# The filter's spectrum in a convolution kernel: its stores move to GpSimd's queue, its swapped copy is made in two halves

## The chip, the cores and the metric

The kernel runs on one core of a Trainium2 chip. The metric is the device time of one execution in microseconds (us), here the median of three runs. One further execution was recorded by the hardware profiler; the traces and pages below are of that one.

## The reference

A long convolution along the sequence by FFT, and then a block that mixes tokens by phases. Batch 8, sequence S = 5696, width 128:

```
Y  = rfft(x, 2S, axis=1) * rfft(h, 2S, axis=0)[None]
y  = irfft(Y, 2S, axis=1)[:, :S]                  # the convolution, 8 x 5696 x 128
theta = y @ w_theta;  zr, zi = y*cos(theta), y*sin(theta)
u  = y + einsum('ts,bsd->btd', w_tok_r, zr) + einsum('ts,bsd->btd', w_tok_i, zi)
out = u + max(u @ w_ch, 0)
```

`w_tok_r` and `w_tok_i` are 5696 x 5696 float32; most of the kernel's time is the product with them.

## The kernel before

The first 365 us or so are the convolution. It works on 8 groups, one after the other: group g is a pair of batches (`bp = g // 2`) and one half of the 128 columns (`dh = g % 2`). Each group goes through four stages, which are woven: stage A of group g+1 runs beside stage C of group g, and stage B of group g+1 beside stage D of group g.

- **Stage A** (`stage_a`) is the first short transform of x, by matmul with the table `f1_t`; ScalarE (L259) or VectorE (L257) evict it into the tile `a`. The pool of `a` has one buffer, so `a` of group 1 (a__1403 in the trace) is written where the filter's spectrum (a__241) was.
- **Stage B** (`stage_b`) runs over 12 chunks of 8 (the last: 2) rows of the first transform. TensorE makes the second transform of a chunk (`f2`, L270), ScalarE evicts it as `xs` (L431, two buffers), and VectorE multiplies it with the filter's spectrum into `uv_t` (L433, or two products at L438 in group 0 and for the short chunk). The spectrum comes in the tile `hs`, four buffers (`LEAD = 4`): `load(c + LEAD)` is issued once chunk c has been multiplied.
- **Stage C** and **stage D** transform back; VectorE and ScalarE evict them as `g` (L460, L458) and `yt` (L493, L495). SyncE stores `yt` to DRAM in eight pieces (L502).

The filter h goes the same way first. Its spectrum, `hst_of(c)`, stays in SBUF in place of its own `a`, with real rows on partitions 0 to 63 and imaginary rows on 64 to 127, for both halves of the columns. Group 0 multiplies by it directly, and by `hs`, in which the two row blocks have been exchanged by a copy from SBUF (L421, two copies of 64 KB for a chunk). The groups from 1 on can't, since the SBUF room goes to `a` of the next group. They read `hf_hbm` in DRAM (L423, 256 KB for a chunk), whose layout is (chunk, column half, 128 rows, straight or exchanged, 512). It is filled in two steps:

- `h_store(n)`, n = 0 to 11, one call behind each of group 0's stage B chunks in program order, writes 64 rows of SBUF (L369): for chunks 0 to 5, 6 to 10 and 11, for each column half and each of real and imaginary. The pieces are 384, 320 and 16 KB. They make rows 0 to 63.
- `swap_rows()` fills rows 64 to 127 with the same data exchanged, by six copies from DRAM to DRAM (L406). Each covers both column halves; with chunk and half merged, the first dimension of the copies is 12, 10 and 2.

Both are issued by SyncE, whose order is made by the scheduler, as is TensorE's: L369, the first L406, group 0's L421 from chunk 4 on, the other L406, the L423 of group 1. VectorE, ScalarE and GpSimd keep the program's order up to the end of group 0's stage C (`ordered`). GpSimd issues the loads of x (L153: 16 pieces for a group, of 160 and 18 KB, each group's loads two groups ahead; from group 2 on, a copy at L151 makes a piece wait for that group's `g`).

A table of sines and cosines for stage D (`e_table`) is made in three parts. ScalarE's two activations of the first part (L195 and L202, called `curves()`) stand behind chunk 5 of group 0's stage B.

The second part of the kernel, from about 365 us on, forms the phases and multiplies by the two large matrices (L1334 and L1234 on TensorE), whose rows GpSimd loads in a ring (L680).

Of the kernel before, what the change touches and what calls it, by code (L numbers as in the profile page):

```python
# [22 lines left out]
def kernel(  # L23
# [10 lines left out]
    nc = tc.nc  # L34
# [63 lines left out]
    hf_hbm = nc.dram_tensor("hf_hbm", (NCK, 2, P, 2, HD * CK), F16, kind="Internal").ap()  # L98
# [5 lines left out]
    def psum():  # L104
        return fp.tile([P, 2, 512], F32, tag="ps", name="ps")
# [244 lines left out]
    def hst_of(c, n=1):  # L350
        c0 = CHK[c][0]
        c1 = CHK[c + n - 1][0] + CHK[c + n - 1][1]
        return a_h["a"].rearrange("p (h k) d -> p h (k d)", h=2)[:, :, c0 * HD:c1 * HD]
# [12 lines left out]
    def h_store(i):  # L366
        i, h, ri = i // 4, i // 2 % 2, i % 2
        c0, c1, w = ((0, NCK // 2, HD * CK), (NCK // 2, NCK - 1, HD * CK), (NCK - 1, NCK, HD * CHK[-1][1]))[i]
        nc.sync.dma_start(hf_hbm[c0:c1, h, :64, ri, :w].rearrange("c p n -> p c n"),  # L369
                          hst_of(c0, c1 - c0)[64 * ri:64 * ri + 64, h].rearrange("p (c n) -> p c n", n=w))  # L370

    r_u = fc.tile([P, P], F16)
    r_v = fc.tile([P, RC], F16)
# [24 lines left out]
            cosine(e_t[:K1, n0:n0 + 11, 0, :], k3)  # L398
        return curves

    def swap_rows():
        for c0, c1, w in ((0, NCK // 2, HD * CK), (NCK // 2, NCK - 1, HD * CK), (NCK - 1, NCK, HD * CHK[-1][1])):
            for ri in range(2):
                dst, src = (hf_hbm[c0:c1, :, r0:r0 + 64, r, :w].rearrange("c h p n -> (c h) p n")
                            for r0, r in ((64, ri), (0, 1 - ri)))
                nc.sync.dma_start(dst, src)  # L406

    def e_minus():
        nc.vector.tensor_scalar(e_neg[:K1], e_t[:K1, 1:2 * NP:2], -1.0, None, op0=mult)
# [1 line left out]
    def stage_b(a_st, dh, warm=WARM, first=False):  # L411

        hs_of = {}

        def load(c):
            if c >= NCK:
                return
            hs = hs_of[c] = fh.tile([P, 2, HD * CK], F16, tag="hs", name="hs")
            w = HD * CHK[c][1]
            for e in range(2 if first else 0):  # L420
                nc.sync.dma_start(hs[64 * e:64 * e + 64, 1, :w], hst_of(c)[64 - 64 * e:128 - 64 * e, dh])  # L421
            if not first:
                nc.sync.dma_start(hs[:, :, :w], hf_hbm[c, dh, :, :, :w])  # L423

        def chunk(c):
            c0, ck = CHK[c]
            hv = hs_of[c][:, :, :HD * ck].rearrange("p r (d k) -> p r d k", k=ck)
            straight = hst_of(c)[:, dh].rearrange("p (d k) -> p d k", k=ck).unsqueeze(1) if first else hv[:, 0:1]
            ps = f2(a_st, c, warm)
            xs = fs.tile([P, 2, HD, CK], F16, tag="xs", name="xs")  # L430
            nc.scalar.activation(xs[:, :, :, :ck], ps, AF.Copy)  # L431
            if ck == CK and not first:
                nc.vector.tensor_tensor(  # L433
                    uv[:, :, :, c0:c0 + ck],
                    xs.rearrange("p e d k -> p e (d k)").unsqueeze(1).to_broadcast([P, 2, 2, HD * CK]),
                    hv.rearrange("p r d k -> p r (d k)").unsqueeze(2).to_broadcast([P, 2, 2, HD * CK]), op=mult)
            for r in range(2 if ck < CK or first else 0):
                nc.vector.tensor_tensor(  # L438
                    uv[:, 2 * r:2 * r + 2, :, c0:c0 + ck], xs[:, :, :, :ck],
                    (hv[:, 1:2] if r else straight).to_broadcast([P, 2, HD, ck]), op=mult)  # L440
            load(c + LEAD)
        return [lambda c=c: load(c) for c in range(LEAD)], [lambda c=c: chunk(c) for c in range(NCK)]

    def stage_c(st, last):

        def chunk(q):
            if q == 0:
                st["g"] = fg.tile([P, 2 * N2, P], F16, tag="g", name="g_")
            ps = psum()
            for i in range(8):  # L450
                o = ps[:, i // 4, (i % 4) * P:(i % 4 + 1) * P]
                at = (q + i) * K1
                nc.tensor.matmul(o, u_t[:, at:at + P], r_u, start=True, stop=False)  # L453
                nc.tensor.matmul(o[:, 2 * NP:], v_t[:, at:at + P], r_v, start=False, stop=True)  # L454
            g_out = st["g"][:K1, :, q:q + 8]
            g_in = ps[:K1].rearrange("p a (q c) -> p c (a q)", q=4)
            if (last and q % 24 == 0) or (not last and q % 32 == 16):
                nc.scalar.activation(g_out, g_in, AF.Copy)  # L458
            else:
                nc.vector.tensor_copy(g_out, g_in)  # L460
        return [lambda q=q: chunk(q) for q in range(0, 2 * HD, 8)]
# [48 lines left out]
    def front(g, by_dve=(), a_=None, spare=None):  # L510
        if g >= len(groups):
            return [], [], []
        bp, dh = groups[g]
        x16 = x16s[g].rearrange("p b n d -> p (b n) d")
        steps, a_st = stage_a(lambda q: x16[:NB, :, q], by_dve, a_, spare)
        return (steps, *stage_b(a_st, dh, 0 if g else WARM // 2, g == 0))
# [141 lines left out]
    def open_ring():  # L658

        ring["all"] = keep.tile([P, K1 * 3 * N2], BF16, tag="keep", name="ring")  # L660
        pump()
# [109 lines left out]
    def with_load(step, load):  # L771
        def both():
            step()
            if load:
                ring["upto"] += 1
                pump()
        return both

    for g, (bp, dh) in enumerate(groups):
        st = {}  # L780
        last = g + 1 == len(groups)
        a_, load_, b_ = fronts.pop(g + 1) if g + 1 in fronts else front(g + 1)
        if last:
            for _ in range(3):
                steps0.pop(0)()
        now = ([with_load(steps0.pop(0), n < 6) for n in range(9)] if last else [], 0.0, 0.88)
        c_ = stage_c(st, last)
        if g == 0:
            ec = []
            swap_rows()  # L790
            now = ([lambda: ec.append(e_table(1)), lambda: ec.pop()(), lambda: ec.append(e_table(2)), lambda: ec.pop()(),
                    e_minus],
                   -0.1, 0.6)
        woven((c_, 0.06 if a_ else 0.0, 1.0), (a_, 0.0, 0.88), now, load_, (load_x(g + 2, st), 0.1, 1.02))
        if g == 0:
            ordered.close()
        if g + 2 == len(groups):
            xin.close()
            open_phases()
            load_ya0()  # L800
        now = [steps0.pop(0) for _ in range(4)] if last else []
        woven((b_, 0.0, 0.8), (stage_d(st, bp, dh, load_ya1 if last else None, g + 2 == len(groups)), 0.08 if b_ else 0.0, 1.1 if b_ else 1.0), now)
        if g + 2 == len(groups):
            load_ya1(st["yt"], True)
            open_ring()
# [332 lines left out]
    for i, (k, p, tt, j0, s0, nj) in enumerate(stretches):  # L1138
# [47 lines left out]
        if tt is None:  # L1186
# [21 lines left out]
            if end_of_pair:  # L1208
# [5 lines left out]
                c, c0 = c_last  # L1214
# [184 lines left out]
```

## Time and profile before

| | us |
|---|---|
| runs | 2031.64, 2032.19, 2037.83 (median 2032.19) |
| profiled execution | 2035.47, its span 2033.7 |
| TensorE busy | 1956.1 (96%) |
| VectorE busy | 1538.2 (76%) |
| ScalarE busy | 636.9 (31%) |
| GpSimd busy | 974.6 (48%) |

Rows of the trace give a start in us from the span's beginning, a duration, the engine, the line of the kernel, the operation and its tiles (out<-in), and in brackets how long the engine had stood idle and what ended that. PE is TensorE, DVE VectorE, ACT ScalarE, POOL GpSimd; SPq is SyncE's queue of DMA issues. A DMA issue has a duration on its queue, and later a landing. The clock in a table of windows is the share of full speed that TensorE was granted.

### The profile page before, as it was taken

The numbers are of one execution on the slowest core, as the hardware profiler recorded it, in microseconds if no ns is written. First come the engines' busy times: TensorE is split into PE (matmuls) and PEld (weight loads), VectorE is DVE, ScalarE is ACT, GpSimd is POOL, SyncE is SP. The second block draws the span as 40 slices with busy tenths as digits, with TensorE's granted clock in tenths as the row PEclk, the third lists the DMA queues.
The fourth block names the chain that finished last, engine by engine and source line by source line (L and its number), as shares of the span: only waits on it lengthen the run. The fifth ranks groups of instructions, "written<-read, shape, count | busy, mean of one in ns | idle before, by whom it ended". The sixth has DMA issues, their size and how long they took to land.

```text
span 2033.7 us, 42627 instructions
## 1 busy us (share of the span) xinstructions
PE 1956.1 (96%) x16297; PEld 1079.9 (53%) x16297; DVE 1538.2 (76%) x2819; ACT 636.9 (31%) x934; POOL 974.6 (48%) x1787
## 2 busy tenths in 40 slices
PE   7799998989999999999999999999999999999998
PEld 5689887644444444444444444444444444444444
DVE  8877787666778787887867668768677786777767
ACT  6777788852233323333300000011111111111111
POOL 8323313575363635454566555453545445354450
PEclk9998999999999999999999999999999999999999
DMA  9999987999798989999999799886978879788793
GB/s 153 161 165 150 152 174 212 254 227 193 152 181 172 178 169 161 185 170 177 168 172 156 119 246 223 133 153 125 153 133 146 150 123 157 129 150 143 133 158 84
DMA packets 508525, 332.48 MB, mean 163 GB/s; under 512 B 186727, under 2 KB 461671, under 8 KB 508231
## 3 DMA queue, kind: packets, MB, share of 16 engines
q0 software_dynamic: 322656, 157.47, 61.0%
q1 hardware_dynamic: 179680, 160.74, 27.2%
q10 hardware_dynamic: 5984, 11.54, 1.6%
q8 instruction: 128, 2.10, 0.4%
q14 instruction: 77, 0.63, 0.1%
HBM read 373.24 MB, written 92.95 MB: 229 GB/s over the span
## 4 chain that ended last, share of the span: by engine, by line
PE 65%; DMA 4%; DVE 2%; POOL 1%; issue 1%; ACT 0%; DVEq 0%; ACTq 0%
PE m L1334 61%; DMA ring<-in_moe_w_tok_i_dram 2%; POOL ring L680 1%; PE v L993 1%; PE utp L986 1%; DVE c L1341 1%; PE m L1338 1%; DVE wt L906 1%; DMA ring<-in_moe_w_tok_r_dram 1%; PE theta_ps L564 0%; PE tpz L934 0%; DMA wl<-in_moe_w_tok_i_dram 0%; DVE b L844 0%; DMA cp_hbm<-c 0%; PE m L1201 0%
## 5 line engine op out<-in xcount | busy, mean ns | idle before, releaser
L680 POOL DMA_DIRECT2D ring<-in_moe_w_tok_i_dram x720 | 387.7, 545 | 675.5 <-DVE wt L906 578.2
L906 DVE STREAM_TRANSPOSE wt<-ring 128x384 f32<-128x384 f32 (+2 forms) x720 | 359.0, 523 | 125.0 <-PE m L1334 77.0
L680 POOL DMA_DIRECT2D ring<-in_moe_w_tok_r_dram x720 | 386.3, 547 | 119.2 <-DVE wt L906 68.3
L1334 PE MATMUL m<-b,wt 128*128 128x512 bf16 x1640 | 388.3, 379 | 1.9 <-DVE wt L906 1.7
L1334 PEld LDWEIGHTS <-wt 128*128 128x128 bf16 x1804 | 176.0, 98 | 215.5 <-DVE wt L906 4.3
L1341 DVE TENSOR_TENSOR c<-c,m 128x512 f32<-128x512 f32 x412 | 265.2, 668 | 0.4 <-PE m L1334 0.4
L988 ACT ACTIVATE ring<-utp 128x512 bf16<-128x512 bf16 x85 | 50.7, 597 | 572.0 <-PE utp L986 572.0
L453 PE MATMUL ps<-r_u,uv_t 128*128 128x128 f16 x1024 | 117.4, 220 | 5.6 <-DVE g__1416 L460 2.0
L1234 PE MATMUL m<-b,wt 128*128 128x512 bf16 x480 | 114.2, 386 | 7.7 <-DMA b<-zz 5.4
L983 ACT ACTIVATE ub<-c 128x512 bf16<-128x512 f32 x88 | 55.2, 628 | 199.7 <-DVE c L1295 118.9
L454 PE MATMUL ps<-r_v,uv_t 128*128 128x100 f16 x1024 | 115.5, 209 | 0.1
L153 POOL DMA_DIRECT2D x<-in_x_dram x128 | 98.1, 773 | 20.7 <-POOL x L151 14.9
L454 PEld LDWEIGHTS <-uv_t 128*128 128x128 f16 x1024 | 100.8, 99 | 7.0 <-issue 5.9
L433 DVE TENSOR_TENSOR uv_t<-xs,hs 128x2048 f16<-128x2048 f16 x77 | 91.5, 1221 | 17.1 <-ACT xs L431 9.8
L453 PEld LDWEIGHTS <-uv_t 128*128 128x128 f16 x1024 | 100.8, 98 | 1.6 <-DVE uv_t L438 1.3
L431 ACT ACTIVATE xs<-ps 128x1024 f16<-128x1024 f32 x96 | 90.7, 972 | 29.2 <-PE ps L270 15.2
L1234 PEld LDWEIGHTS <-wt 128*128 128x128 bf16 x528 | 51.0, 99 | 67.1 <-issue 12.4
L566 ACT ACTIVATE red<-theta_ps,magic 128x512 f32<-128x512 f32 (+1 forms) x46 | 31.6, 687 | 153.1 <-PE theta_ps L564 92.9
L270 PEld LDWEIGHTS <-w_t 64*128 64x128 f16 x3240 | 56.5, 98 | 32.6 <-issue 24.3
L936 ACT ACTIVATE ring<-tpz 128x512 bf16<-128x512 bf16 (+1 forms) x46 | 27.4, 597 | 137.0 <-PE tpz L934 122.5
L250 PE MATMUL ps<-f_t,x 89*128 89x180 f16 x512 | 64.5, 258 | 0.7 <-DVE a L257 0.5
L995 DVE SCALAR_TENSOR_TENSOR c<-v,c 128x512 f32<-128x512 f32 x88 | 59.8, 682 | 2.8 <-PE v L993 2.1
(2932 smaller groups left out, 3765.3 us busy)
## 6 DMA issues: line engine op xcount, KB each, us to landing
ring<-in_moe_w_tok_r_dram POOLq DMA_DIRECT2D x352, 96.0 KB, 4.6
ring<-in_moe_w_tok_i_dram POOLq DMA_DIRECT2D x352, 96.0 KB, 4.9
ring<-in_moe_w_tok_r_dram POOLq DMA_DIRECT2D x352, 80.0 KB, 4.5
ring<-in_moe_w_tok_i_dram POOLq DMA_DIRECT2D x352, 80.0 KB, 4.0
cp_hbm<-c SPq DMA_DIRECT2D x88, 256.0 KB, 2.4
c<-cp_hbm SPq DMA_DIRECT2D x88, 256.0 KB, 3.7
out_dram<-c SPq DMA_DIRECT2D x88, 256.0 KB, 4.3
hs<-hf_hbm SPq DMA_DIRECT2D x77, 256.0 KB, 3.6
```

The source lines that it names most:

```text
L153: nc.gpsimd.dma_start(x16[p0:p1, e, n0:n0 + 16, :HD], bass.AP(tensor=src.tensor, offset=src.offset + (p0 * N2 + n0) * D + dh * HD, ap=[[N2 ...
L250: nc.tensor.matmul(ps[:, i // 2, (i % 2) * 2 * K1:(i % 2 + 1) * 2 * K1], lhs(q + i), f1_t[:NB], start=True, stop=True)
L431: nc.scalar.activation(xs[:, :, :, :ck], ps, AF.Copy)
L433: nc.vector.tensor_tensor(uv[:, :, :, c0:c0 + ck], xs.rearrange("p e d k -> p e (d k)").unsqueeze(1).to_broadcast([P, 2, 2, HD * CK]), hv. ...
L453: nc.tensor.matmul(o, u_t[:, at:at + P], r_u, start=True, stop=False)
L454: nc.tensor.matmul(o[:, 2 * NP:], v_t[:, at:at + P], r_v, start=False, stop=True)
L680: nc.gpsimd.dma_start(wb[32 * i:32 * i + 32, :ng, :nj * 64], bass.AP(tensor=a.tensor, offset=a.offset + row0 * S + p * H + i * QR + j0 * 6 ...
L906: nc.vector.transpose(wt.rearrange("p j t r -> p (j t r)").bitcast(F32).rearrange("p (j g t) -> p g j t", j=TJ, g=4)[:, :ng, :nj], wb[:, : ...
L995: nc.vector.scalar_tensor_tensor(c[:m], v[:m], 0.0, c[:m], op0=ALU.max, op1=ALU.add)
L1234: nc.tensor.matmul(ms[n // 2 * 2 + h], a[n][:, j, :, r], bts_of[p][jj][n % 2 * 2 + h][:, r, :], start=(n % 2 == 0 and jj == 0 and r == 0), ...
L1334: nc.tensor.matmul(ms[q], a[q][:, j, :, r], bts[jj][q][:, r, :], start=(jj == 0 and r == 0), stop=(jj == NJ - 1 and r == 1 and q not in left))
L1341: nc.vector.tensor_tensor(c, z, ms[q], op=op)
```

## The change

GpSimd, and no longer SyncE, issues the twelve stores of `h_store`. In its program order they stand behind the loads of x for group 1 and the making of the identity, and ahead of the loads of x for group 2. `swap_rows` takes a column half: half 1, which group 1 reads, is called at the beginning of group 0's loop step, half 0, which group 2 reads, at that of group 1's. The copies of each are held in SyncE's order behind the load of `hs` that was issued last by then (`tc.issue_after`): chunk 11 of group 0 for half 1, chunk 11 of group 1 for half 0. There are twelve copies of half the size in place of six; their first dimension is 6 or 5, and for the last chunk 64.

```diff
     def h_store(i):
...
-        nc.sync.dma_start(hf_hbm[c0:c1, h, :64, ri, :w].rearrange("c p n -> p c n"),
-                          hst_of(c0, c1 - c0)[64 * ri:64 * ri + 64, h].rearrange("p (c n) -> p c n", n=w))
+        nc.gpsimd.dma_start(hf_hbm[c0:c1, h, :64, ri, :w].rearrange("c p n -> p c n"),
+                            hst_of(c0, c1 - c0)[64 * ri:64 * ri + 64, h].rearrange("p (c n) -> p c n", n=w))
...
-    def swap_rows():
+    hs_last = {}
+
+    def swap_rows(h):
         for c0, c1, w in ((0, NCK // 2, HD * CK), (NCK // 2, NCK - 1, HD * CK), (NCK - 1, NCK, HD * CHK[-1][1])):
             for ri in range(2):
-                dst, src = (hf_hbm[c0:c1, :, r0:r0 + 64, r, :w].rearrange("c h p n -> (c h) p n")
-                            for r0, r in ((64, ri), (0, 1 - ri)))
-                nc.sync.dma_start(dst, src)
+                dst, src = (hf_hbm[c0:c1, h, r0:r0 + 64, r, :w] for r0, r in ((64, ri), (0, 1 - ri)))
+                with tc.issue_after(hs_last["load"]):
+                    nc.sync.dma_start(dst, src)
...
             for e in range(2 if first else 0):
-                nc.sync.dma_start(hs[64 * e:64 * e + 64, 1, :w], hst_of(c)[64 - 64 * e:128 - 64 * e, dh])
+                hs_last["load"] = nc.sync.dma_start(hs[64 * e:64 * e + 64, 1, :w],
+                                                    hst_of(c)[64 - 64 * e:128 - 64 * e, dh]).ins
             if not first:
-                nc.sync.dma_start(hs[:, :, :w], hf_hbm[c, dh, :, :, :w])
+                hs_last["load"] = nc.sync.dma_start(hs[:, :, :w], hf_hbm[c, dh, :, :, :w]).ins
...
         c_ = stage_c(st, last)
+        if g == 1:
+            swap_rows(0)
         if g == 0:
             ec = []
-            swap_rows()
+            swap_rows(1)
```

## The prediction

> **What bounds the kernel now.** I read the page first. Its chain of work that ended last begins at 529 us and is matmul time almost throughout:
>
> ```profile
> PE 65%; DMA 4%; DVE 2%; POOL 1%; issue 1%; ACT 0%; DVEq 0%; ACTq 0%
> ```
>
> The change lies in the first 130 us, ahead of that chain. There each stage waits for the one before it, so a stall counts at the end only if it delays the hand-over from group to group; I take one that does to move all that follows. I went to VectorE's timeline (start, duration, what runs, idle time and its releaser):
>
> ```profile
> 54.27 0.69 DVE L438 TENSOR_TENSOR uv_t<-xs,a__241 128x1024 f16<-128x1024 f16 x1
> 58.61 0.69 DVE L438 TENSOR_TENSOR uv_t<-xs,hs 128x1024 f16<-128x1024 f16 x1 [3.64 <-DMA hs<-a__241]
> ...
> 60.48 0.69 DVE L438 TENSOR_TENSOR uv_t<-xs,a__241 128x1024 f16<-128x1024 f16 x1
> ...
> 88.18 1.22 DVE L460 CAST g__1416<-ps 90x1024 f16<-90x1024 f32 x1 [0.38 <-PE ps L454]
> 90.91 1.08 DVE L493 CAST yt<-ps 128x890 bf16<-128x890 f32 x1 [1.51 <-PE ps L489]
> 91.92 2.35 DVE L433 TENSOR_TENSOR uv_t<-xs,hs 128x2048 f16<-128x2048 f16 x2
> ...
> 129.18 1.22 DVE L460 CAST g__2476<-ps 90x1024 f16<-90x1024 f32 x1 [0.38 <-PE ps L454]
> 130.82 2.36 DVE L433 TENSOR_TENSOR uv_t<-xs,hs 128x2048 f16<-128x2048 f16 x2 [0.41 <-ACT xs L431]
> ```
>
> In group 0 VectorE stands 3.64 us for chunk 4's copy into hs, though chunk 0 freed that buffer at 50.64 (its second product starts at 49.95 and takes 0.69). SyncE's own queue shows why:
>
> ```profile
> 33.66 18.43 SPq L369 DMA_DIRECT2D hf_hbm<-a__241  x12
> 52.14 0.90 SPq L406 DMA_DIRECT2D hf_hbm<-hf_hbm  x1
> 53.14 12.18 SPq L421 DMA_DIRECT2D hs<-a__241  x16
> 65.36 8.37 SPq L406 DMA_DIRECT2D hf_hbm<-hf_hbm  x5
> 73.84 35.20 SPq L423 DMA_DIRECT2D hs<-hf_hbm  x16
> ```
>
> The twelve stores of the spectrum hold the queue until 52.1 and a 768 KB swap goes ahead, so chunk 4's copy is issued at 53.14 behind that swap's data.
>
> **The change part by part.** *Stores off SyncE.* Chunk 4's two copies can go out at 50.7 and 51.3 (0.595 us each, the median of L421). Landing took 1.7 to 4.6 us over all L421, so the second lands between 53.0 and 55.9; VectorE needs it at 54.9. Between nothing and 1 us of the wait is left. But ScalarE is next in line:
>
> ```profile
> 54.42 1.02 ACT L431 ACTIVATE xs<-ps 128x1024 f16<-128x1024 f32 x1 [0.18 <-DVE uv_t L438]
> 55.34 1.10 ACT L195 ACTIVATE e_t<-e_turns,zero_b 90x979 f16<-90x979 f32 x1
> 56.35 1.11 ACT L202 ACTIVATE e_t<-e_t,half_pi 90x979 f16<-90x979 f32 x1
> 59.42 1.02 ACT L431 ACTIVATE xs<-ps 128x1024 f16<-128x1024 f32 x1 [1.96 <-DVE uv_t L438]
> ```
>
> The sine and cosine stand in ScalarE's fixed order between chunk 5 and chunk 6. Chunk 6's eviction cannot start before about 57.4 and ends at 58.4; VectorE's chunk 6 then starts at 58.4 instead of 60.48. The gain is 2.05 us, not 3.64: the table replaces the DMA. It also covers the remaining 0 to 1 us of the copy's wait.
>
> *Stores on GpSimd.* It is free where they land in its order:
>
> ```profile
> 46.02 0.29 POOL masks.py:199 TENSOR_SCALAR_AFFINE_SELECT ident_bf<-ident_bf 128x128 bf16<-128x128 bf16 x1
> 71.06 0.18 POOL L151 COPY x<-g__1416 1x1 f16<-1x1 f16 x1 [24.75 <-DVE g__1416 L460]
> ...
> 91.28 4.41 POOL L153 DMA_DIRECT2D x<-in_x_dram  x7 [0.21 <-issue]
> ```
>
> Twelve issues at 0.60 (the 9-row pieces of x) to 0.91 us (the 80-row pieces) are 7 to 11 us inside 24.75 us of idleness; the x pieces behind them are not delayed. The stores begin 12.6 us later than now, at 46.3. Their 2.88 MB went at about 270 GB/s between 48 and 52 us, and beside 1 MB of hs copies end near 46.3 + 3.9/0.27 = 61. What waits for that is ScalarE's first write of the next `a` (67.08 now, 65 then), which reuses the buffer they read. Margin 4 us: cost nothing; if the cover is gone, a stall of ScalarE one for one.
>
> [...] The row at 91.28 is 0.63 us per issue while VectorE runs L433, 2048 elements in 1.22 us, twice the rate per element of L460 (1024 in 1.22); elsewhere the same pieces take 0.60. [...]
>
> *The swap in halves.* Each half is 1.44 MB, with first dimension 6 or 5 chunks where it was 12 or 10. The DMA view from 69 to 73 us has the end of the 12-block copy, then the 10-block one (busy tenths of the 16 engines, GB/s):
>
> ```profile
> DMA  6887888878878866856957767668568567676676
> GB/s 246 307 307 256 307 297 287 297 276 287 307 266 287 297 246 236 287 205 246 430 205 256 256 225 256 236 225 287 205 225 287 205 246 266 225 256 236 225 256 236
> ```
>
> First about 0.75 at 290, then 0.62 at 245: twelve and ten sixteenths, 24.5 GB/s per leading block. So I estimate 147 and 123 GB/s for 6 and 5 blocks, 2.7 us per big copy and 10.7 us per half, where the whole now takes about 11. [...]
>
> The first half goes out near 62 and ends near 75; the hs loads behind it are needed at 90. Cost nothing. The second half sits in SyncE's order as one copy behind group 1's last hs load (105), then the eight yt stores (107.4 to 112.5), then the other five, and only then group 2's first four hs loads, which now go out by 109. In them, each of the first five engines moves 192 KB of big swaps and 64 KB of hs after 112.5: 10.4 us at 24.5 KB/us alone, to 123. But x loads run from 113 on. If the queue gets 55% (an estimate: x moves 160 KB every 2.2 us here, 73 GB/s, and up to 160 GB/s at 91 us), it is 18.9 us: the first hs lands at 129 to 130, the fourth at 132. VectorE wants the first at 130.9 and the others 1.2 us apart. Cost: nothing by a hair; bounds 0 and 4.5 us (at 10.6 KB/us per engine: 250 GB/s from 38 to 46 us, less x's 81, over 16).
>
> *Order.* The built program's instruction lists differ elsewhere in one place: in group 2's stage B, VectorE takes the yt copy ahead of its first two products, and ScalarE one too, as group 1 does now. From the last g copy's start to the end of stage B group 1 takes 108.70 − 88.18 = 20.52, less 1.21 of DMA waits 19.3; group 2 takes 147.92 − 129.18 = 18.74. Cost 0.57; with the waits 1.8.
>
> *Sum.* −2.05 + 0.57 = −1.5 us. On the profiled execution's 2035.47 (span 2033.7) that is 2034.0. That execution lies 3.3 above the median of 2032.19, so the prediction for a median is 2030.7.
>
> **The rivals.** *The halves run on too few engines (slower).* Group 2's hs comes late by 3.6 to 4.5 us, and PE then sits idle. The windows grant PE 0.50 after such gaps (106 to 113, 174 to 185 us); in group 1 the third g copy comes 7.17 us after stage B's end, in group 2, without it, 4.42: 2.75 more. Total −1.5 + 4.5 + 2.75 = +5.8 or 2038, up to 2041 if a second group is drawn in. It decides once the fourth swap copy ends after about 127. For it: 0.62 busy, and a margin of 1 us. Against: x fills half the capacity only. Chance 0.30, of which 0.19 beyond 0.3%.
>
> [...] Chance 0.07.
>
> *More than one stall goes (faster).* Group 1's 1.21 us of hs waits and its half-clock stretch (2.75) vanish with the earlier hand-over, and the new order costs nothing: −2.05 − 1.21 − 2.75 = −6.0, and another group's stretch could go too: 2026. For it: the stretches come in some groups only and not in others alike. Chance 0.17.
>
> *It does not do what it says.* The stores' data, now beside the copies, hold chunk 4 as long as the swap did: no gain, 2032 to 2034. Against it: 4.6 us is the slowest L421. Chance 0.08.
>
> **How the numbers follow.** My forecast keeps 0.38. A measurement of this kernel can tell about 0.3% (6.1 us) from no change, since three runs spread over 6.2 us. Slower: 0.19 + 0.06 + 0.02 = 0.27; faster 0.17; same 0.38 + 0.11 + 0.01 + 0.06 = 0.56. Range 2024 to 2040: it holds the forecast's bounds (2.05 at best, 4.5 lost), most of the few-engine case and most of the faster one. The forecast alone would be 2028 to 2034.
>
> **What would show it.** Right: chunk 4's copies issued by 51, no DMA wait of over 1 us ahead of chunk 4's second product, chunk 6 at 58.4 behind the cosine, stage B ending near 65.3; 12 L369 rows on GpSimd between 46 and 61; swap copies at 5 to 6 sixteenths of the engines. Wrong: a DMA wait of L433 in group 2, a store landing after 65, or the clock's 0.50 stretches in other groups than now by more than one.

## The result, and the profile after

The changed kernel is slower: 2040.61 us median of 11 runs (2034.06 to 2049.31) against 2031.87 of 11 runs of the kernel before beside them (2025.72 to 2037.83). The ratio is 1.0056, 95% interval 1.0039 to 1.0072: 8 to 15 us, more than the 0.3% that can be told apart. The profiled execution took 2048.64 (span 2046.9) and is among the slowest of its runs, so its 13.2 us more of span are not the mean loss. Lines of the kernel have moved by two to five: L421 is now L423, L423 is L426, L406 is L408, L433 is L436, L438 is L441, L431 is L434, L460 is L463, L493 is L496, L453 is L456, L502 is L505.

The chain that ended last is what it was, matmuls of the second part:

```profile
PE 66%; DMA 3%; DVE 3%; issue 1%; POOL 1%; ACT 0%; ACTq 0%; DVEq 0%; SPq 0%; POOLq 0%
```

VectorE's timeline of the changed kernel in group 0 and in group 2 (start, duration, what runs, in brackets the idle time ahead of it and its releaser):

```profile
53.92 0.69 DVE L441 TENSOR_TENSOR uv_t<-xs,a__241 128x1024 f16<-128x1024 f16 x1
59.74 0.69 DVE L441 TENSOR_TENSOR uv_t<-xs,hs 128x1024 f16<-128x1024 f16 x1 [5.13 <-DMA hs<-a__241]
60.35 0.69 DVE L441 TENSOR_TENSOR uv_t<-xs,a__241 128x1024 f16<-128x1024 f16 x1
62.25 0.69 DVE L441 TENSOR_TENSOR uv_t<-xs,hs 128x1024 f16<-128x1024 f16 x1 [1.22 <-DMA hs<-a__241]
...
133.49 1.08 DVE L496 CAST yt<-ps 128x890 bf16<-128x890 f32 x1 [1.45 <-PE ps L492]
138.04 2.36 DVE L436 TENSOR_TENSOR uv_t<-xs,hs 128x2048 f16<-128x2048 f16 x2 [3.47 <-DMA hs<-hf_hbm]
140.84 2.36 DVE L436 TENSOR_TENSOR uv_t<-xs,hs 128x2048 f16<-128x2048 f16 x2 [0.44 <-ACT xs L434]
144.49 1.23 DVE L436 TENSOR_TENSOR uv_t<-xs,hs 128x2048 f16<-128x2048 f16 x1 [1.29 <-DMA hs<-hf_hbm]
146.64 4.82 DVE L436 TENSOR_TENSOR uv_t<-xs,hs 128x2048 f16<-128x2048 f16 x4 [0.92 <-DMA hs<-hf_hbm]
```

The wait for chunk 4's copy, 3.64 before, has not gone: it is 5.13, and chunk 5's is 1.22. In group 2, where VectorE waited for no hs before, it waits 3.47 + 1.29 + 0.92 = 5.68. Chunk 4's copies did go out as early as forecast. SyncE's queue from 50 to 56 us, and GpSimd's timeline:

```profile
50.35 5.79 SPq L423 DMA_DIRECT2D hs<-a__241  x4
```

```profile
46.18 6.42 POOL L369 DMA_DIRECT2D hf_hbm<-a__241  x9 [0.24 <-issue]
52.90 0.54 POOL L369 DMA_DIRECT2D hf_hbm<-a__241  x1 [0.31 <-DMA hf_hbm<-a__241]
55.13 0.53 POOL L369 DMA_DIRECT2D hf_hbm<-a__241  x1 [1.69 <-DMA hf_hbm<-a__241]
56.49 0.53 POOL L369 DMA_DIRECT2D hf_hbm<-a__241  x1 [0.83 <-DMA hf_hbm<-a__241]
```

Four copies of 64 KB kept SyncE's queue for 5.79 us: the first 0.46, the other three 1.5 to 2.0 each, where the median of all is 0.60. The second copy of chunk 4 was issued from 50.85, and VectorE had it at 59.74. GpSimd's twelve stores were issued between 46.2 and 57.0. The DMA view from 50 to 62 us has what the engines did (busy tenths, GB/s, then packets, MB and share of the 16 engines of each queue; q0 is GpSimd's, q1 SyncE's):

```profile
DMA  5996969999979899999999998999999667473755
GB/s 191 287 218 137 232 205 328 300 314 246 273 259 300 259 341 341 358 365 379 307 321 304 280 300 300 331 376 311 301 263 290 178 164 208 123 184 92 195 133 130
...
q0 software_dynamic: 855, 2.54, 71.9%
q1 hardware_dynamic: 663, 0.55, 17.3%
```

From about 52 to 59 us the 16 engines are nearly full, with 2.54 MB of the stores and 0.55 MB of copies between them in the twelve us. That is the first loss. For the second, SyncE's queue over the whole stretch:

```profile
66.87 9.75 SPq L408 DMA_DIRECT2D hf_hbm<-hf_hbm  x6
76.78 31.85 SPq L426 DMA_DIRECT2D hs<-hf_hbm  x12
108.69 0.76 SPq L408 DMA_DIRECT2D hf_hbm<-hf_hbm  x1
113.17 5.32 SPq L505 DMA_DIRECT2D yt_hbm<-yt  x8
118.59 10.09 SPq L408 DMA_DIRECT2D hf_hbm<-hf_hbm  x5
128.78 26.88 SPq L426 DMA_DIRECT2D hs<-hf_hbm  x16
```

The five swap copies behind the yt stores hold the queue for 10.09 us, so group 2's first hs load goes out at 128.78. The two of 320 KB take 3.6 us each of it, the others 0.5 to 1.2. The first half, at 66.87, harms nobody: group 1 waits 0.25 for hs, where it waited 1.21 before.

TensorE's clock is lower in both places. In group 0 the kernel before has 0.61 and 0.54 of it from 58 to 66 us, the changed one 0.50; from 70 to 78 the changed one still has 0.64 and 0.51, the kernel before 1.00. Windows of 4 us in group 2 (the first of the last three columns is the granted clock), the changed kernel first and then the kernel before, which has 1.00 in all of them:

```profile
132.00:136.00 4.00, 2.07 (x78) 1.91 (x80) 1.12 (x2) 1.33 (x2) 0.91 (x1) 1.00 1.43 283
136.00:140.00 4.00, 2.95 (x48) 2.75 (x50) 1.96 (x2) 1.02 (x2) 0.59 (x1) 0.50 1.23 109
...
152.00:156.00 4.00, 3.50 (x51) 3.44 (x51) 3.31 (x5) 2.82 (x5) 0.00 (x0) 0.63 0.54 149
```

```profile
136.00:140.00 4.00, 2.74 (x107) 2.59 (x108) 2.85 (x4) 2.55 (x4) 0.00 (x0) 1.00 0.76 164
...
152.00:156.00 4.00, 4.00 (x73) 3.99 (x70) 3.53 (x3) 3.35 (x6) 1.98 (x4) 1.00 1.25 223
```

**Where the 13.2 us of the two profiles arise**, from the ends of the stages on VectorE (after less before): end of group 0's stage B 69.8 − 67.3 = +2.5; end of its stage C +5.1; end of group 1's stage C +1.6, where the kernel before had a clock of 0.55 from 106 to 113 and the changed one 1.00; end of group 2's stage B 155.3 − 147.9 = +7.4; end of its stage C +10.2; end of the last group's +13.3. In these two profiles nothing of it is given back behind the convolution.

### The profile page after: what moved, and what is told of

The parts are those of the page before. It is cut to its first block, busy times and chain, and to the rows that moved or that the text cites. A ratio compares the mean times of both kernels' runs of the same rounds, so it can differ in the third digit from the quotient of the medians.

```text
span 2046.9 us, 42652 instructions
## 1 busy us (share of the span) xinstructions
PE 1963.1 (96%) x16297; PEld 1088.6 (53%) x16297; DVE 1538.3 (75%) x2819; ACT 637.0 (31%) x934; POOL 983.0 (48%) x1799
## 4 chain that ended last, share of the span: by engine, by line
PE 66%; DMA 3%; DVE 3%; issue 1%; POOL 1%; ACT 0%; ACTq 0%; DVEq 0%; SPq 0%; POOLq 0%
PE m L1339 62%; DMA b<-z_hbm 2%; DVE c L1346 1%; PE v L998 1%; PE utp L991 1%; PE m L1343 1%; DVE wt L911 1%; DMA ring<-in_moe_w_tok_r_dram 1%; POOL ring L683 1%; PE theta_ps L567 0%; PE tpz L939 0%; DVE b L849 0%; PE m L1206 0%; DMA yT<-yt_hbm 0%; DMA wl<-in_moe_w_tok_i_dram 0%
## 5 line engine op out<-in xcount | busy, mean ns | idle before, releaser
L456 PE MATMUL ps<-r_u,uv_t 128*128 128x128 f16 x1024 | 119.6, 223 | 6.3 <-DVE g__1416 L463 2.5
L1239 PE MATMUL m<-b,wt 128*128 128x512 bf16 x480 | 112.5, 383 | 6.7 <-DMA b<-zz 4.1
L436 DVE TENSOR_TENSOR uv_t<-xs,hs 128x2048 f16<-128x2048 f16 x77 | 91.3, 1222 | 20.6 <-DMA hs<-hf_hbm 10.4
L456 PEld LDWEIGHTS <-uv_t 128*128 128x128 f16 x1024 | 102.2, 100 | 1.9 <-DVE uv_t L441 1.7
L434 ACT ACTIVATE xs<-ps 128x1024 f16<-128x1024 f32 x96 | 90.4, 972 | 31.9 <-PE ps L270 13.2
L270 PEld LDWEIGHTS <-w_t 64*128 64x128 f16 x3240 | 60.6, 102 | 33.6 <-issue 25.2
```

The source lines that it names most:

```text
L270: nc.tensor.matmul(ps[:, e, j * HD:(j + 1) * HD], w_t2[rows, c0 + j, N2 * (1 - ri):N2 * (3 - ri)], a_st["a"][rows, ri * K1 + c0 + j, :], s ...
L436: nc.vector.tensor_tensor(uv[:, :, :, c0:c0 + ck], xs.rearrange("p e d k -> p e (d k)").unsqueeze(1).to_broadcast([P, 2, 2, HD * CK]), hv. ...
L1239: nc.tensor.matmul(ms[n // 2 * 2 + h], a[n][:, j, :, r], bts_of[p][jj][n % 2 * 2 + h][:, r, :], start=(n % 2 == 0 and jj == 0 and r == 0), ...
```

## The experiments

The letters in the quoted texts name theories; each text says what its theory expects. Times are medians beside the kernel before on the same chip, ratios with their 95% intervals. Labels with "rows" are versions in which a swap copy's first dimension is 64 rows and not 6 or 5 chunks.

### The two halves of the change, each alone

**e1**: the changed kernel with 64 rows in front.

```diff
-                dst, src = (hf_hbm[c0:c1, h, r0:r0 + 64, r, :w] for r0, r in ((64, ri), (0, 1 - ri)))
+                dst, src = (hf_hbm[c0:c1, h, r0:r0 + 64, r, :w].rearrange("c p n -> p c n") for r0, r in ((64, ri), (0, 1 - ri)))
```

> The changed kernel with one edit: the halves' copies name the 64 rows as their first dimension, not the 6 or 5 chunks; bytes and calls stay. Theory A (two separate losses: the stores beside group 0's copies, and copies that keep to 5 or 6 of the 16 DMA engines): the copies show the share of nearly all engines and over 200 GB/s, group 2's hs lands before VectorE asks for it (the 3.47 us and the waits of 1.29 and 0.92 behind it go), group 0's wait stays at 6 us, and the time lies 3 to 6 us above the kernel before. Rival B (group 2's hs is late by its place behind the yt stores and by x's loads, whatever the engines): group 2's wait stays above 2 us and the time at +7 to +10.

2035.65 against 2030.56, ratio 1.0035 (1.0020 to 1.0050). Group 2 waits for no hs; group 0 still waits 5.60:

```profile
132.33 2.37 DVE L436 TENSOR_TENSOR uv_t<-xs,hs 128x2048 f16<-128x2048 f16 x2 [0.67 <-ACT xs L434]
```

The copies held SyncE's queue for 0.54 to 0.63 us each. But in group 1 VectorE now waits 2.69 for hs.

**e2**: the changed kernel with the stores back on SyncE (`nc.gpsimd` to `nc.sync` at L369).

> The changed kernel with the stores issued by SyncE again; the halves stay as they are, behind group 0's copies. Theory A: group 0's copies now follow the stores directly, at 52.1, with no 768 KB copy ahead; chunk 4's wait is 0.5 to 1.5 us (3.64 before, 5.13 and 1.22 after), stage B of group 0 ends near 65.5, and group 2's wait of 3 to 6 us stays: 1 to 5 us above the kernel before. Rival C (nearly all of the loss is the stores on GpSimd): at or below the kernel before.

2042.35, ratio 1.0058 (1.0037 to 1.0078). Group 0 waits 1.26, group 2 waits 6.48. SyncE's queue and VectorE's first product of group 2:

```profile
107.07 5.30 SPq L505 DMA_DIRECT2D yt_hbm<-yt  x8
112.41 10.33 SPq L408 DMA_DIRECT2D hf_hbm<-hf_hbm  x5
122.85 1.95 SPq L426 DMA_DIRECT2D hs<-hf_hbm  x4
```

```profile
132.03 4.68 DVE L436 TENSOR_TENSOR uv_t<-xs,hs 128x2048 f16<-128x2048 f16 x4 [3.57 <-DMA hs<-hf_hbm]
```

**e3**: the kernel before with the stores on GpSimd, whole swaps.

> The kernel before with one edit: the stores on GpSimd; the six whole copies stay where the scheduler puts them (one of them now ahead of chunk 9's copies). Theory A: group 0's wait is 5 to 7 us, its stage C has a half-clock stretch behind it, group 2 does not wait, and the time is 3 to 6 us above the kernel before. Rival B' (all of the loss comes from the halves): within 1 us of it.

2034.03, ratio 1.0021 (1.0006 to 1.0036). Group 0 waits 7.76 in three places; the last is new, chunk 9's copy behind a swap that has now overtaken it. Group 2 waits 0.55. VectorE's row and SyncE's queue:

```profile
70.11 0.69 DVE L438 TENSOR_TENSOR uv_t<-xs,hs 128x1024 f16<-128x1024 f16 x1 [3.40 <-DMA hs<-a__241]
```

```profile
62.70 1.69 SPq L406 DMA_DIRECT2D hf_hbm<-hf_hbm  x1
64.51 3.70 SPq L421 DMA_DIRECT2D hs<-a__241  x6
```

That is 4.1 us more of waits than before, and the runs are 1 to 7 us slower. In the profile, which is of the fastest of the twelve runs, group 0's stage C ends 5.6 us later than before, and group 3's at the same time. So a stall in group 0 does not move all that follows in every execution.

**e4**: both undone in their harmful part: stores on SyncE, halves with 64 rows in front, held behind the hs loads.

> The changed kernel with both edits: stores on SyncE, rows first in the halves' copies. Theory A: neither wait is left, chunk 4 waits 0.5 to 1.5 us and group 2 not at all; 1 to 4 us below the kernel before, since the table on ScalarE caps what group 0 gains at 2.05. If the gain is given back by half-clock stretches elsewhere: within 2 us of the kernel before, with the stretches in other groups.

2029.89, ratio 0.9999 (0.9984 to 1.0013). So what is left of the change costs nothing and gains nothing that can be measured. With e1, e2 and the change this makes a square:

| ratio to before | 64 rows in front | 6 or 5 chunks in front |
|---|---|---|
| stores on SyncE | e4 0.9999 | e2 1.0058 |
| stores on GpSimd | e1 1.0035 | the change 1.0056 |

Alone, the stores cost about 7 us (0.35%) and the shape and place of the copies about 12; each is clear of e4. Together they cost no more than the latter alone, and the intervals of e1 and of the change overlap, so what the stores add to the copies is not settled. The versions with 64 rows also have VectorE's order of the kernel before in group 2, two products ahead of the yt copy; the change, e2 and e9 have the yt copy first.

In e4's profile group 0's stage B has no hs wait, and what took its place is the table on ScalarE, as forecast (VectorE, then ScalarE):

```profile
60.98 0.69 DVE L441 TENSOR_TENSOR uv_t<-xs,a__241 128x1024 f16<-128x1024 f16 x1 [1.62 <-ACT xs L434]
```

```profile
57.93 1.10 ACT L195 ACTIVATE e_t<-e_turns,zero_b 90x979 f16<-90x979 f32 x1
58.93 1.11 ACT L202 ACTIVATE e_t<-e_t,half_pi 90x979 f16<-90x979 f32 x1
59.94 1.91 ACT L434 ACTIVATE xs<-ps 128x1024 f16<-128x1024 f32 x2
```

One reason for the missing gain is to be seen one group later. In group 1 e4 waits 2.40 us for hs, where the kernel before waits 0.76 + 0.45 = 1.21 in two places:

```profile
101.11 3.60 DVE L436 TENSOR_TENSOR uv_t<-xs,hs 128x2048 f16<-128x2048 f16 x3 [2.40 <-DMA hs<-hf_hbm]
```

All versions with 64 rows in front and no added matmuls wait there for 2.4 to 3.5 us; why, no run here settles. In e4's profile, which is the slowest of its twelve runs, group 2's stage B has in addition a granted clock of 0.50 from 136 to 144 us without any wait for hs.

### Is it the stores' data? Half of them

**e7**: e1 without column half 0's six stores and its swap; the groups from 1 on all read half 1.

```diff
     def h_store(i):
...
+        if h == 0:
+            return
```

> The changed kernel with rows first, and six of the twelve stores left out, those of column half 0, with its swapped rows; all groups from 1 on multiply by half 1. Theory A1 (chunk 4's copies are late because the stores' data fill the DMA engines from 50 to 60): the stores end near 52 to 54, and chunk 4's wait falls from 5 to 0 to 2 us. Rival A2 (a GpSimd queue in use slows SyncE's issues whatever the bytes): the issues still take 1.5 to 2 us and the wait stays above 3.

One run, 2034.06 where before has 2030.04. The wait is one of 2.51 us, less than half of e1's 5.60 but more than expected:

```profile
57.92 0.69 DVE L443 TENSOR_TENSOR uv_t<-xs,hs 128x1024 f16<-128x1024 f16 x1 [2.51 <-DMA hs<-a__241]
```

With e2 (the same copies, the stores issued by SyncE from 33 us on: 1.26) this points to the stores' data in those 12 us. Half the stores is also half of GpSimd's issues; but here the last of them ended at 51.2, and the engines stayed nearly full until about 55.

### Engines or place? The second half of the swap

**e8**: e1 with all six copies of the second half held behind group 0's yt stores. **e9**: the changed kernel with its 6- and 5-chunk copies, all six ahead of those stores.

```diff
-                with tc.issue_after(hs_last["load"]):
+                with tc.issue_after(hs_last["load" if h else "yt"]):
```

> The changed kernel with rows first, and all six copies of the second half held behind group 0's yt stores, where in the changed kernel one stood ahead of them. Theory B1 (the number of engines decides): they end by 122 although they start later, and group 2 waits for no hs, or for under 1 us. Rival B2 (the place behind yt decides): group 2's wait is 2 us or more.

> The changed kernel with the 6- and 5-chunk copies as they are, but all six ahead of group 0's yt stores. Theory B1 alone (engines): 10.7 us from about 109 on, to 120, with group 2's wait of 3 to 6 us still there in most of its size. Rival B2 (place): no wait of over 1 us. If both count: 1 to 3 us.

One run each: 2034.53 and 2043.54 (before 2030.04). SyncE's queue, e8 and then e9:

```profile
114.11 6.12 SPq L505 DMA_DIRECT2D yt_hbm<-yt  x8
120.34 5.60 SPq L408 DMA_DIRECT2D hf_hbm<-hf_hbm  x6
127.95 27.43 SPq L426 DMA_DIRECT2D hs<-hf_hbm  x16
```

```profile
107.30 8.94 SPq L408 DMA_DIRECT2D hf_hbm<-hf_hbm  x6
116.33 7.51 SPq L507 DMA_DIRECT2D yt_hbm<-yt  x8
123.89 31.42 SPq L426 DMA_DIRECT2D hs<-hf_hbm  x16
```

Group 2 waits 2.68 in e8 and not at all in e9. So the number of engines alone, my first theory, is not it: six slow copies do no harm there when they go early, and quick ones do some when they go late. In e1 the scheduler itself had put four of the six ahead of the yt stores, so its cure was part shape and part place. e9's own time is as bad as the change's; it keeps group 0's wait (5.86). In its profile 2.3 us more are lost between the ends of stage C in groups 1 and 2 without a wait for hs, beside a mean granted clock of 0.982 over the whole execution; one run can't say more.

### Does the table cap the gain?

**e11**: e4 with the first sine and cosine behind chunk 11 of group 0's stage B (`if n == 5:` to `if n == 11:`).

> The stores on SyncE and the halves of the swap with 64 rows in front (the run before that had no hs wait in group 0), and now ScalarE's first sine and cosine stand behind chunk 11 of group 0's stage B instead of behind chunk 5. Theory (the table, not a DMA, limited what the freed wait could give): VectorE's 1.62 us of idle time ahead of chunk 6 is gone, no idle time over 0.7 us is left between chunk 0 and chunk 11, and from chunk 0's first product to the end of stage B takes 14.3 us (15.9 less 1.6); the two activations then run at the end of stage B, beside or ahead of the writes of the next a, which begin no later than now. Time 1.6 us below that run, 2028, if the group behind keeps it. Rival (something else is late at chunk 6, a copy of hs or TensorE's matmuls): an idle time of over 1 us remains in chunks 6 to 8 and the stage still takes 15.5 or more; time as that run, 2030.

2031.26 against 2025.13, ratio 1.0011 (0.9991 to 1.0031): no gain. The 1.62 us is gone, but the stage takes 15.89 us, as e4's 15.88. In this execution the stage began at 48.68, in e4's at 51.93; the stores leave SyncE's queue at 51.5 and 51.3, so here chunk 4 waits for its copy again:

```profile
55.49 0.69 DVE L441 TENSOR_TENSOR uv_t<-xs,hs 128x1024 f16<-128x1024 f16 x1 [1.18 <-DMA hs<-a__241]
```

The theory holds in its first half (the table was what VectorE stood for), and fails in its second: the next thing is late at once.

### TensorE's clock

In all versions the time of single executions goes with the mean granted clock: over some 260 runs, each taken from its version's mean, 1.1 us less for each 0.001 more (correlation −0.71). The changed kernel's runs have a mean clock of 0.983, those of before 0.988 to 0.989. I tried to hold the clock by added work.

**e5** and **e10**: e4 with two, or one, matmuls of 512 columns ahead of every stage B chunk from group 1 on.

```diff
         ps = psum()
+        for n in range(ahead):
+            nc.tensor.matmul(ps[:, n % 2], w_t2[:, 2, :P], w_t2[:, 2:6].rearrange("p k n -> p (k n)")[:, :512],
+                             start=True, stop=True)
```

> The kernel with both edits (stores on SyncE, rows first), and in groups 1 to 7 two further matmuls of 512 columns ahead of each chunk of stage B, into the PSUM columns that the chunk then overwrites: 24 per group, 0.43 us per chunk at full clock. Theory D (what makes a wait of 2 us cost 4, and what spreads the runs, is TensorE's half clock after idle stretches): fewer half-clock stretches behind stage B of groups 1 to 7, a mean granted clock of 0.990 or more (0.987), 2 to 6 us less than without them. Against D: TensorE's extra 5 us per group lies on the path, and the time rises by 5 to 20.

> As the run with two added 512-column matmuls ahead of every stage B chunk from group 1 on (stores on SyncE, halves with 64 rows in front), but with one. The two filled TensorE (17.99 of 18 us) and made each group 39.0 to 39.6 us long, with the granted clock at full from group 1 on. Theory D (idle stretches of TensorE are followed by a granted clock of 0.50, which is what makes the difference between executions): with one, TensorE's added work is half, some 0.2 us a chunk at full clock; if the idle stretches are still short enough, the half clock stays away in groups 1 to 7 (less than 6 us lost, against 31 without any), groups take 37 to 38.5, and the time is 2022 to 2034. Rival (added matmuls cost what they take, whatever the clock): half of what two cost, +7 us, 2037 with the clock between. Second rival (one is too little to keep the clock): half-clock stretches as without, over 20 us lost, time 2033 to 2038.

e5: 2044.03, ratio 1.0076 (1.0056 to 1.0095). The half-clock stretches behind group 0 are gone (mean clock 0.993, e4's 0.987), but TensorE is full (17.99 of 18 us) and a group takes 39 us. e10: 2034.54, ratio 1.0037 (1.0018 to 1.0056). I count as lost to the clock the length of each window times what is missing to a granted clock of 1. The convolution of e10's profile ended 9 us earlier than e4's, at a mean clock of 0.988 over the whole execution against 0.983, yet the span was the same 2035.9: by that count 12.0 us were lost between 365 and 475 us, against 1.8. Neither pays.

**e12** and **e13**: the changed kernel and the kernel before with one such matmul.

> The changed kernel with one added 512-column matmul ahead of every stage B chunk from group 1 on; the kernel before with the same addition runs beside it. Theory D (of the changed kernel's loss, about half is its longer waits for hs, the rest the granted clock of 0.50 that follows the longer idle stretches): with the clock held up in both, the two differ by 4 to 7 us, where the kernels without the addition differ by 9 to 12; less than 18 us are lost to the clock between 30 and 380 us, against 36. Rival (the waits alone make the loss, the clock only scatters the runs): the two still differ by 9 to 12 us.

> The kernel before with one added 512-column matmul ahead of every stage B chunk from group 1 on. The addition alone cost 2 to 9 us on another version (ratio 1.0037, 1.0018 to 1.0056). If it costs the same here, 2030 to 2038; it is the yardstick for the changed kernel with the same addition.

e12: 2047.24, ratio 1.0091 (1.0071 to 1.0112). e13: 2030.90, ratio 1.0015 (0.9999 to 1.0030). They differ by 16 us, not by 4 to 7: my theory failed in this form. The added matmul raised the mean clock by 0.004 in both (from 0.988 to 0.992 in e13, from 0.983 to 0.987 in e12), so the gap of 0.005 between them stayed. Between these two profiles the shift is +1.5 at the end of group 0's stage B, +4.8 at the end of its stage C, +10.6 at the end of group 2's stage B, and +12.6 at the end of the last group. So 10.6 of it are there by group 2, and 3.3 of that in group 0's stage C, ahead of the first added matmul.

**e17, e18, e19**: the disputed cost by itself, in the kernel before: a stall of 5.9 us of VectorE in group 2's stage B; the same with TensorE given work meanwhile; that work alone.

```diff
-            if ck == CK and not first:
+            for _ in range(0 if ck < CK or first else 1 + stall if c == 2 else 1):
                 nc.vector.tensor_tensor(
```

> The kernel before, with VectorE's product of chunk 2 in group 2's stage B made six times in place of once (the same result written again): VectorE is 5.9 us late there (5 x 1.18), as it is in the changed kernel by its 5.68 us of waits for hs in that stage; no DMA, store or copy is changed. Theory H (a stall in one stage costs more than its length, because TensorE's idle time in it is followed by a granted clock of 0.50): 8 to 12 us slower than before, as the version that has the 6.48 us of waits in that stage and 1.26 in group 0 lost 11.8. Rival I (a stall moves everything behind it by its length and no more): 5 to 7 us. Rival K (later groups take some of it back): 4 us or less.

> The same stall of 5.9 us, with nine added 512-column matmuls ahead of each of chunks 3, 4 and 5 of that stage, so that TensorE has 5.9 us of work of its own (27 x 0.22 at full clock) while VectorE is late. Theory H: the cost falls to 5 to 7 us, and the granted clock stays above 0.9 in the 15 us behind the stall. Rivals I and K: no change against the stall without them, or a few us more.

> Control: the 27 added matmuls without the stall. They take 5.9 us of TensorE at full clock, of which what is not hidden in its idle time is paid: 0 to 6 us slower than before under every theory.

| | ratio | stage C of group 2 behind it, us |
|---|---|---|
| e17 stall | 1.0045 (1.0028 to 1.0061) | 22.3 |
| e18 stall, filled | 1.0059 (1.0037 to 1.0081) | 19.0 |
| e19 filling alone | 1.0037 (1.0019 to 1.0056) | 19.4 |
| before | 1 | 19.0 |

Windows of TensorE behind the stall, e17 and then e18 (granted clock third from the end):

```profile
144.00:148.00 4.00, 3.90 (x61) 3.62 (x56) 4.00 (x5) 3.48 (x5) 0.00 (x0) 0.50 0.63 165
148.00:152.00 4.00, 4.00 (x47) 4.00 (x45) 1.39 (x3) 2.69 (x5) 0.00 (x0) 0.50 0.56 178
```

```profile
144.00:148.00 4.00, 2.93 (x71) 2.83 (x69) 4.00 (x4) 3.50 (x5) 0.00 (x0) 1.00 0.42 124
148.00:152.00 4.00, 3.96 (x65) 3.68 (x65) 2.92 (x5) 3.63 (x6) 0.45 (x2) 1.00 0.82 251
```

In e17's profile the stall of 5.9 us is followed by a clock of 0.50, and the next stage C takes 3.3 us more; with work in the gap (e18) the clock stays at 1.00 and it does not. In e17's profile stage B of group 2 itself grew by 4.2 us (21.3 against 17.1), since 1.6 us in which VectorE had stood idle before are gone. That makes 7.5 with stage C, where the ratio says 9 us (6 to 12): more than the bare 4.2, but the bare 5.9 is not excluded. As times, e18 missed its expectation (a cost of 5 to 7 us; it was 12), since the filling costs 7.5 by itself, more than the 6 allowed, and saves less; its profile is of the fastest of its six runs. So what the half clock adds is seen in the profiles and not shown as a time. The change's own stage C there took 21.8 us, e2's 21.5; versions without a wait in that stage took 19.0 to 19.6 (e5, with TensorE full, 20.1). e12, which waits 5.05 there but has a matmul added to every chunk, took 19.1, as theory H would have it. In between it is not clear-cut: e8 (2.68 of waits) took 19.3, e14 (2.93) 21.5.

### What did not come out: a PSUM buffer in group 0

From the end of stage B to the end of stage C group 0 takes 22.1 us before and 24.7 after, and 24.7 to 25.4 in e1, e8, e9 and e12, but 21.9 to 22.6 in e2, e3, e4, e7, e10, e11 and e13. In the built programs of the first set, and in none of the second, the second g tile is given the PSUM buffer of the first, which VectorE must copy out; the others take one that ScalarE frees. TensorE's timeline of the changed kernel:

```profile
73.48 0.26 PE L456 MATMUL ps<-r_u,uv_t 128*128 128x128 f16 x1 [2.52 <-DVE g__1416 L463]
```

**e14, e15, e16**: the change, e1 and the kernel before, with group 0's stage C starting one chunk of stage A earlier, which undoes that assignment.

```diff
-        woven((c_, 0.06 if a_ else 0.0, 1.0), (a_, 0.0, 0.88), ...
+        woven((c_, (0.0 if g == 0 else 0.06) if a_ else 0.0, 1.0), (a_, 0.0, 0.88), ...
```

> The changed kernel; in group 0 alone the first chunk of stage C stands one chunk of stage A earlier in program order. In the built program TensorE's second g tile of group 0 then takes a PSUM buffer that ScalarE freed (as in the kernel before), and not the one that VectorE's first g copy must free (as in the changed kernel, where TensorE stands 2.52 us for it and the next 5 us run at a granted clock of 0.50). Theory F (this assignment of a buffer is a loss of its own, some 2.6 us in the profile: 24.7 us from the end of stage B to the end of stage C in group 0 where the kernel before takes 22.1): that stretch takes 22 to 22.8 us, no wait of TensorE for the first g copy ahead of the second g tile, and the time is 2 to 4 us below the changed kernel's, 2037 to 2039. Rival G (the longer stretch is the half clock after group 0's wait for hs, whoever frees the buffer): it still takes 24 or more, time as the changed kernel's, 2041.

> The changed kernel with 64 rows as the first dimension of the swap's copies (2035.65 in its own run, 24.7 to 25.1 us from the end of stage B to the end of stage C in group 0) and with the same earlier chunk of stage C in group 0. Theory F: that stretch falls to 22 to 22.8, time 2032 to 2034: what is left above the kernel before is group 0's wait for hs. Rival G: stretch 24 or more, time 2035 to 2036.

> Control: the kernel before with the same earlier chunk of stage C in group 0. Its second g tile takes a buffer that ScalarE freed, with and without. Both theories: 22 to 22.8 us from the end of stage B to the end of stage C in group 0, time as before within 2 us. If it is 2 us or more faster, the move is a gain by itself and has to be taken off the other two.

2045.72, ratio 1.0079 (1.0060 to 1.0097); 2038.96, 1.0041 (1.0025 to 1.0056); 2031.70, 1.0007 (0.9992 to 1.0023). The stretch took 24.1, 25.0 and, in the control, 25.6 us: TensorE's wait for the first g copy is gone, but VectorE's third g copy waits 1.4 to 2.2 us for TensorE. The test does not decide between buffer and clock. It shows that this stretch is not the loss by itself: with it as long in the control as in the change, the change is still 14 us slower.

## Why the prediction was wrong, step by step

- **"The second lands between 53.0 and 55.9 … between nothing and 1 us of the wait is left": the first step that failed.** Issue at 50.35 and 50.85 was right. Issue time (0.595) and landing (1.7 to 4.6) came from rows in which SyncE's queue had its own data alone, and the median hid two of the 24: beside the 768 KB swap, chunk 4's own second copy took 1.37 us to issue and one at 57.0 took 1.90. Beside the stores, the five copies issued from 50.85 to 57.7 took 1.4 to 2.0 us each, and the second was there at 59.74. The same paragraph's neighbour had the stores' data on all engines up to 61; I charged it to ScalarE's writes, which wait for the stores, and not to the copies among them. The term was −2.05 and became +2.5. The rival that names this cause, "the stores' data, now beside the copies, hold chunk 4 as long as the swap did", had 0.08; they hold it longer, 5.13 against 3.64. In the DMA view above, from 50 to 62 us, the packets of GpSimd's queue took 71.9% of the 16 engines' time and those of SyncE's 17.3%.
- **The table in place of the DMA: right as a mechanism.** e4: 15.9 us from chunk 0 to the end of stage B against 67.3 − 49.3 = 18.0, so 2.1 as forecast, with 1.62 behind the cosine. But its stage began later and gave the copies time, e11 shows the next wait, and over its runs e4 gains nothing.
- **GpSimd's stores: right.** First at 46.18 (forecast 46.3), 0.53 to 1.08 us each in its timeline (0.60 to 0.91), ScalarE's first write of `a` (69.59) not held by them: what ended ScalarE's idle time there was VectorE's product. The chance of 0.07 (0.06 of it in the sum for slower) was for stores held while VectorE runs its products. No run shows such a term: nine of the twelve were issued from 46.18 to 52.60, VectorE's L441 products ran from 49.01 to 54.61 without a break, and the last three waited for a DMA.
- **The halves' speed: right.** The copies with 6 and 5 chunks in front went at 139 to 148 GB/s, then 119 to 131 but for one slice, for 147 and 123 estimated, with 0.3 to 0.4 of the 16 engines busy all but once. The DMA view from 68 to 78 us, busy tenths and GB/s:

```profile
DMA  0212323434344444444444444433353334599999
GB/s 0 12 25 66 66 57 106 147 139 147 139 143 147 143 147 148 143 143 143 143 143 147 143 147 147 147 127 119 119 188 123 119 125 131 139 202 213 227 223 208
```

- **"Cost: nothing by a hair; bounds 0 and 4.5 us": the second step that failed.** 5.68 us, beyond the upper bound. The yt stores went out at 113.2 to 118.5 and not at 107.4 to 112.5, since group 0's loss had moved them; but that is not the reason, for in e2 they went out at 107.1 to 112.4, as forecast, and group 2 waits 6.48. Counted from the end of these stores, the sum had the first hs there after 16.5 to 17.5 us (129 to 130 less 112.5), and VectorE asking for it after 18.4 (130.9). In the changed kernel VectorE asked after 16.1 (134.57) and had it after 19.6 (138.04); in e2 after 16.1 and 19.7. So the supply was 2 to 3 us later and the demand 2.3 us earlier than in the sum, against a margin of 1 us, and the waits for later chunks (2.21) come on top. On the supply side the sum had priced the copies' data on the engines. It let the hs loads go out right behind the copies, while the five copies held the queue itself for 10.09 us, where e8's six with 64 rows took 5.60; and the last big one, issued at 124.4, landed 12.5 us later, at 136.9. How much of the 2 to 3 us is queue and how much data stays open.
- **Half the clock behind a stall: only in a rival.** 2.75 was put there; 2.8 was measured (21.8 against 19.0). It belongs in the sum beside the change's 5.68 us and e17's 5.9 (22.3 against 19.0). Behind e8's 2.68 us stage C took 19.3, though the clock was 0.50 from 140 to 144 there; behind e14's 2.93 it took 21.5. "The halves run on too few engines" (0.30, 2038 up to 2041) holds the median, and the wait in group 2 came as it said. But in e9 the same copies, issued ahead of the yt stores, left group 2 without a wait, and the rival still counted a gain of 2.05 in group 0, where there was a loss. That its time fits is in part luck.
- **"I take one that does to move all that follows": not settled.** e3's 4.1 us more of waits cost 1 to 7 us and e17's 5.9 cost 6 to 12, so both intervals hold the bare length; but in e3's profile the later groups took it back.
- **Order in group 2.** VectorE takes the yt copy first, as read from the lists (the row at 133.49). Its 0.57 can't be told from the wait behind it: from the last g copy's start to the end of stage B, e9 with the new order took 21.0 us and e1 with the old one 20.9, both without a wait for hs, where the kernel before took 18.74. The lists also gave the PSUM buffers, which the forecast did not use.

Open: some 3 us that the profiles add behind group 2, and how much of the mean loss is clock; by the slope, the clock's 0.005 would go with about 6 us of it, but stalls and clock come together in the runs, and e12 failed to part them.

## What to carry to other kernels

Moving the stores' issues to an idle queue moved their data in time (issues from 33.66 on before, from 46.18 on after): ask which small, urgent transfers run in the new interval, and price those with full engines (here 1.4 to 2.0 us for an issue, and about 9 us from the start of an issue to use where the kernel before had 5). Here a copy with 6 or 5 chunks in front cost its queue as well as its data (the first half held SyncE's queue for 9.75 us, and from 70 to 76 us the engines were mostly 0.3 to 0.4 busy), so ask what stands behind such a copy in the queue. VectorE's stall of 5.9 us in e17 had a clock of 0.50 behind it for 12 us: look for such a stretch behind a stall, and do not take the cheap end of a bound whose margin is 1 us.

## What the runs showed of the hardware

- With the DMA engines nearly full, SyncE's issue of a 64 KB copy took 1.4 to 2.0 us (the five issued from 50.85 to 57.7 in the changed kernel), and 0.46 to 0.64 in the rest of that trace; in the kernel before two of 24 took 1.37 and 1.90 beside a 768 KB copy, the others 0.50 to 0.63. So the queue is held, not only the data.
- GpSimd's last three stores each waited for an earlier store to land (0.31, 1.69, 0.83 us), with nine issued.
- A stall of 5.9 us that leaves TensorE with half its time idle (2.14 of 4 us busy from 136 to 140 in e17) was followed by a clock of 0.50 from 140 to 152, and adding 27 matmuls kept it at 1.00 there (e18). In the least busy 2 us between 128 and 150 us of e17, from 136 to 138, TensorE had 0.64 us of work.
